# Pooled attention and a SiLU layer on one core: the first denominators two steps later, h sums in halves, another block order at the end, the last product by token halves

## The chip, the cores and the metric

The kernel runs on one core of one Trainium2 chip. The metric is the device time of one execution in microseconds (us). Three executions of the kernel before took 281.76, 282.05 and 282.42 us; the median is 282.05. TensorE is called PE, VectorE DVE, ScalarE ACT, GpSimd POOL and SyncE SP, as in the profile; PEld is PE's loading of weights.

## The reference

Eight batches with eight heads of 576 positions of 64 features. Keys and values are averaged over groups of 8 positions (72 pooled positions), then softmax attention, then a two-layer network on the 4608 rows of 512 features:

```
k_p, v_p = mean of k, v over groups of 8 positions
attn     = softmax(q @ k_p^T / sqrt(64));   x = (attn @ v_p) as [4608, 512]
h        = x @ w_in                         # [4608, 2048]
out      = (h * sigmoid(h)) @ w_out         # [4608, 512], float32
```

## The kernel before, in words

**Tiles.** The 4608 rows are nine token tiles of 512 (t = 0 to 8). While the network works on tile t, the attention of batch a = t + 1 is computed beside it, for tiles up to 6 (a < B = 8). Tiles 7 and 8 have no attention beside them; they are called bare.

**Seven products.** From tile 1 on, both layers use the seven-product form of the 2 x 2 block product (Winograd's form of Strassen). The first layer has four units a, b, c, d, each of seven products numbered 1 to 7; "a5" in the order strings is product 5 of unit a (L575 `unit_product`). The second layer has products P1 to P7 with eight blocks of depth (kt), written as "P5 Q5": P5 is kt 0 to 3, Q5 is kt 4 to 7 (L588 `out_product`). For each kt there are two matmuls of 128x256, one for each token half c of a 256-token block. One such kt, like one output half of a unit product, is a *step*.

**Accumulators.** Each of the second layer's products adds into one of three PSUM banks: o_psA (products 1, 2), o_psE (5, 3), o_psB (6, 7, 4). Between them stand operations of other engines (L601 `behind`): after product 1, DVE copies o_psA into o_psB (L605); after product 5, ACT copies o_psE into an SBUF tile p (L608); after product 6, DVE writes o_psE = o_psB + p (L610). Results go to SBUF in L632 `second`: L635 (product 2), L637 (product 3), L641 (product 7) and L646 (product 4). L482 `store` issues the output DMAs, most of them from SP's queue.

**Banks.** PSUM has eight banks in two rotating pools: "mm" with 3, "at" with 5 (L89). o_psA, o_psB and o_psE and the units' u_psB take from "mm"; u_psA, u_psE and everything of the attention take from "at".

**Sums of h.** The activated first layer lies in h_T. The seven-product form needs four sums of blocks of it, h_sum 0 to 3, made by DVE in `hidden_sum` (L532, instructions at L537). Product 5 reads sum 0, product 6 sum 1, product 7 sum 2, product 3 sum 3. Sum 1 needs sum 0, and sum 3 needs sum 1. Sum 0 needs, for its second half (kt 4 to 7), the activation of product d4, the last of the first layer.

**The order of the work.** All engines run their instructions in the program's order. The order of PE's products is a string (FOUR, BARE, THREE at L768 to L779). The rest are *fillers*, given with a step number: `spread` (L396) issues a filler with number s after the matmuls of step s, before those of step s + 1. In tile 1 (order THREE) most numbers are 2 higher. In tiles 2 to 6, steps 54 to 61 are product 1, 62 and 63 d4, 64 to 71 product 2, 72 to 79 product 5, 80 to 87 product 6, 88 to 95 product 7. In the bare tiles product 1 is 52 to 59, d3 and d4 60 to 63, P2 64 to 67, product 5 68 to 75, product 6 76 to 83, Q2 84 to 87, product 7 from 88.

**Attention in three visits.** For each third of the positions (a *visit*), `scores` (L322) makes 16 matmuls (L330) and four exponentials on ACT (L338, tile es), `denominators` (L342) four matmuls of ones with es (L348), then on ACT ln (L357) and exp(-ln) (L358), and `numerators` (L361) matmuls (L374) and products on DVE (L383) that give xT of the next tile. Ahead of the first scores of a tile, ACT loads another function table (L390), and at the tile's end it loads the other back (L393). Scores of the three visits are at steps 63, 75, 94 and denominators at 75, 87, 103 (L882); numerators of the first visit, and in tiles 2 to 6 those of the third visit of the batch before, at 87.

**The end.** In tile 8 product 7 is added and stored (L641), then product 3 (L637), then product 4 is copied by DVE (L646) and stored by two DMAs, one for each 128 tokens, one from SP's and one from ACT's queue. All stores of tile 8 are single DMAs, since its rows are contiguous.

Of the kernel before, what the change touches and what calls it, by code (L numbers as in the profile page):

```python
# [27 lines left out]
FP32 = mybir.dt.float32  # L28
# [8 lines left out]
def kernel(  # L37
# [11 lines left out]
    B, H, S, D = q.shape  # L49
# [5 lines left out]
    KF = d_model // 128  # L55
    KG = d_ff // 128
    NTT = 512
    NT = NTOK // NTT
    HS = S // 2

    KQ, NQ, CQ = KG // 2, NTT // 2, d_model // 2
# [29 lines left out]
    def ps_tile(shape, dtype, tag, name):  # L91
        return psum.tile(shape, dtype, tag=tag, bufs=banks[tag], name=name)
# [303 lines left out]
    def spread(fillers, n):  # L396
        todo = sorted(fillers, key=lambda f: f[0])
        for i in range(n):
            yield i
            while todo and todo[0][0] <= i:  # L400
                todo.pop(0)[1]()
        for f in todo:
            f[1]()
# [146 lines left out]
    def left(n, kt, c):  # L550
        cs = slice(128 * c, 128 * (c + 1))
        if n in S_OF:
            return h_sum[S_OF[n]][:, kt, cs]
        return h_block(*A_OF[n], kt, kt + 1)[:, 0, cs]
# [4 lines left out]
    def f32_tile(tag, bufs):  # L559
        return mid.tile([128, 2, 256], FP32, tag=tag, bufs=bufs, name=tag)  # L560

    def tile_products(t, order, fillers, last=False):
        order = order.split()
        step = spread(fillers, sum(KF if it[0] == "g" else 4 if it[0] in "PQ" else 2 for it in order))
        add = ALU.add
        tt, vcopy, acopy = nc.vector.tensor_tensor, nc.vector.tensor_copy, nc.scalar.copy
        ps, f32 = {}, {}

        def bank(y, b):
            tag = "mm" if y == "o" or b == "B" else "at"  # L570
            ps[y, b] = ps_tile([128, 2, 256], FP32, tag, f"{'o' if y == 'o' else 'u'}_ps{b}")

        BANK = {1: "A", 2: "A", 5: "E", 3: "E", 6: "B", 7: "B", 4: "B"}

        def unit_product(y, n):  # L575
            if n in (1, 5):
                bank(y, BANK[n])
            w, x = unit_weights(y, n), unit_x(t, n)
            for u in range(2):
                next(step)  # L580
                for kk in range(2):
                    nc.tensor.matmul(  # L582
                        ps[y, BANK[n]][:, u, :], lhsT=w[:, kk, 128 * u : 128 * (u + 1)],
                        rhs=x[:, kk, :], start=n in (1, 5) and u == 0 and kk == 0,
                        stop=kk == 1, skip_group_check=True,
                    )

        def out_product(n, k0, k1):  # L588
            if n in (1, 5) and k0 == 0:
                bank("o", BANK[n])  # L590
            w = right(n)
            for kt in range(k0, k1):
                next(step)
                for c in range(2):
                    nc.tensor.matmul(  # L595
                        ps["o", BANK[n]][:, c, :], lhsT=left(n, kt, c), rhs=w[:, kt, :],
                        start=n in (1, 5) and kt == 0 and c == 0,
                        stop=kt == KQ - 1, skip_group_check=True,
                    )

        def behind(y, n):  # L601

            if n == 1:
                bank(y, "B")
                vcopy(out=ps[y, "B"], in_=ps[y, "A"])  # L605
            elif n == 5:
                f32[y] = f32_tile("p5", 3)
                acopy(f32[y], ps[y, "E"])  # L608
            elif n == 6:
                tt(out=ps[y, "E"], in0=ps[y, "B"], in1=f32[y], op=add)  # L610

        def hidden(y, i, j, src):
            g = UNITS[y][i]
            nc.scalar.activation(  # L614
                h_T[:, g : g + 2, j * NQ : (j + 1) * NQ], src, func=AF.Silu
            )

        def unit(y, n):
            unit_product(y, n)
            behind(y, n)  # L620
            if n == 2:
                hidden(y, 0, 0, ps[y, "A"])
            elif n == 3:
                hidden(y, 1, 0, ps[y, "E"])
            elif n == 7:
                c22 = f32_tile("c22", 2)
                tt(out=c22, in0=ps[y, "B"], in1=f32[y], op=add)  # L627
                f32[y, 2] = c22
            elif n == 4:
                hidden(y, 0, 1, ps[y, "B"])  # L630

        def second(n):  # L632
            behind("o", n)
            if n == 2:
                vcopy(out=o_sb[0][:, :, LO], in_=ps["o", "A"])  # L635
            elif n == 3:
                vcopy(out=o_sb[0][:, :, HI], in_=ps["o", "E"])  # L637
                for c in range(2):
                    store(t, c, FULL)
            elif n == 7:  # L640
                tt(out=o_sb[1][:, :, HI], in0=ps["o", "B"], in1=f32["o"], op=add)  # L641
                if last:
                    for c in range(2):
                        store(t, 2 + c, HI)
            elif n == 4:
                (vcopy if last else acopy)(o_sb[1][:, :, LO], ps["o", "B"])  # L646
                for c in range(2):
                    if last:
                        store(t, 2 + c, LO, (both[c],))
                    else:  # L650
                        store(t, 2 + c, FULL)

        for it in order:
            if it[0] == "g":
                plain(t, step, int(it[1:]), 0, NTT)
            elif it[0] in "PQ":
                h = it[0] == "Q"
                out_product(int(it[1]), 4 * h, 4 * h + 4)
                if h:
                    second(int(it[1]))  # L660
            else:
                y = "abcd".index(it[0])
                if it[1] == "s":
                    hidden(y, 1, 1, f32.pop((y, 2)))
                else:
                    unit(y, int(it[1]))
        for _ in step:
            pass
# [95 lines left out]
    def load_half_2(name, half):  # L764
# [6 lines left out]
        " cs d3 c4 " + HEAD  # L771
    )
    BARE = FOUR[: FOUR.index("d3")] + (
        "c4 P1 ds Q1 d3 d4 P2 P5 Q5 P6 Q6 Q2 P7 Q7 P3 Q3 P4 Q4"
    )
    THREE = (
        "g0 g1 g2 g3 b1 b5 c1 c5 b6 b2 c6 c2 b7 b3 c7 c3 bs d1 d5 b4 cs c4 d6 d2 P1 d7 d3 Q1"
# [4 lines left out]
    for t in range(NT):  # L782
        a = t + 1
# [40 lines left out]
            continue  # L824

        order = ORDER.get(t, FOUR if a < B else BARE)
        o = 2 if t == 1 else 0
        f = []

# [3 lines left out]
        def late(s, fn, *args, **kw):  # L833
            at(s + o, fn, *args, **kw)
# [6 lines left out]
        else:  # L841
            late(43, hidden_sum, 2, 0, 4)
            late(53, hidden_sum, 2, 4, 8)
        late(64, hidden_sum, 0, 0, 4)
        late(65, hidden_sum, 0, 4, 8)
        late(66, hidden_sum, 1, 0, 8)
        late(88 if t == 1 else 76, hidden_sum, 3, 0, 8)
        if t == 1:
            for i in range(PW):
# [1 line left out]
        if a < B:  # L851
            if t == 1:
                for j in range(2):
                    at(14, slot_sums, "k", j, halves=True)
                    at(30, select_k, 2, j)
                    at(31, copy_k, 2, j)
                    late(66, slot_sums, "v", j, halves=True)
                for fn in (select_v, copy_v):
                    for j in range(2):
                        late(82, fn, 2, j, *(("at",) if fn is select_v else ()))  # L860
                at(15, load_one, 3, "k")
                at(15, load_q, 3)
                at(16, load_rest, 3, "k")
                late(64, load_one, 3, "v")
                late(66, load_rest, 3, "v")
            else:
                at(0, behind_x_sums)
                at(0, pool_k, a)
                if a + 1 < B:
                    at(0, load_one, a + 1, "k")  # L870
                at(1, pool_v, a)
                if a + 1 < B:
                    at(1, load_one, a + 1, "v")
                    at(2, load_q, a + 1)
                    at(3, load_rest, a + 1, "k")
                    at(4, load_rest, a + 1, "v")
                at(34, k_transpose, a)
            q_at = (24, 25, 26, 60) if t == 1 else (22, 32, 47, 67)
            for n in range(4):
                at(q_at[n], q_transpose, a, n % 2, n // 2)  # L880
            late(63, attn_tables)
            for n, (sc, den) in enumerate(zip((63, 75, 94), (75, 87, 103))):  # L882
                late(den, denominators, a, visits[n])
                late(sc, scores, a, visits[n])
            nu_at = (87, 103, 106)
            for n, sg in enumerate(visits):
                if n < 2 or t >= B - 2:
                    late(nu_at[n], numerators, a, sg)
                if n == 0 and 1 < t < B - 1:
                    late(nu_at[n], numerators, a - 1, visits[2])  # L890
# [33 lines left out]
```

## Time and profile before

| stage (us from the span's start) | length, us | PE busy | DVE busy | ACT busy |
|---|---|---|---|---|
| tile 2, 82.12 to 110.98 | 28.86 | 28.80 | 21.68 | 22.25 |
| tile 3, 110.98 to 139.84 | 28.86 | 28.80 | 21.75 | 22.26 |
| tile 4, 139.84 to 168.71 | 28.87 | 28.82 | 22.41 | 22.25 |
| tile 5, 168.71 to 197.51 | 28.80 | 28.75 | 21.70 | 22.26 |
| tile 6, 197.51 to 226.87 | 29.36 | 29.30 | 22.54 | 22.25 |
| tile 7, 226.87 to 251.65 | 24.78 | 24.78 | 17.76 | 13.06 |
| tile 8, 251.65 to 276.45 | 24.80 | 24.79 | 16.29 | 13.06 |
| end, 276.45 to 280.60 | 4.15 | 0.00 | 0.69 | 0.00 |

The profiled execution took 282.42 us; its span, from first to last instruction, is 280.60, with 1.82 around it. The clock granted to PE is full (1.00) in all these stages. Matmuls overlap, so a row of the timeline that gives "1.91 us x16" is a product whose successor starts 1.75 us after it. The timeline gives start, duration, engine, line, operation, and in brackets how long the engine had been idle before it and what ended that.

### The profile page before, as it was taken

What the parts mean: (1) busy time and instruction counts of PE and PEld (TensorE: products, weight loads), DVE (VectorE), ACT (ScalarE), POOL (GpSimd) and SP (SyncE); (2) the same over time, 40 slices, a digit from 0 to 9 for tenths busy, and PEclk for the clock granted to TensorE, in tenths of its full rate; (3) what the DMA queues carried; (4) which work ended last, traced back from release to release, by engine and by line L of the source; (5) the groups of instructions that cost most, each with busy time, mean ns of one, the idle gap of its engine ahead of it and who ended that gap; (6) DMA issues with size and microseconds to landing.
All of it is one profiled execution on the core that took longest, in us unless ns stands there. A gap on an engine that the chain in (4) does not pass through costs nothing.

```text
span 280.6 us, 7263 instructions
## 1 busy us (share of the span) xinstructions
PE 272.3 (97%) x2952; PEld 211.8 (75%) x2959; DVE 209.3 (75%) x377; ACT 190.5 (68%) x375; POOL 97.4 (35%) x102
## 2 busy tenths in 40 slices
PE   8889999999999999999999999999999999999994
PEld 4348544488788878887888778877887788888883
DVE  4787777887897867876787687777787687766762
ACT  1677766568669785978498858885798578319700
POOL 8565116342138510962087229850900000000000
PEclk9999999999999999999999999999999999999999
DMA  7999999896646896569546966998410032004004
GB/s 212 274 250 239 207 309 183 244 194 112 137 66 145 220 166 114 134 164 167 93 109 180 171 93 162 182 106 128 121 31 0 4 90 62 2 25 124 5 2 150
DMA packets 31473, 37.72 MB, mean 134 GB/s; under 512 B 10352, under 2 KB 22384, under 8 KB 31440
## 3 DMA queue, kind: packets, MB, share of 16 engines
q0 software_dynamic: 23792, 26.64, 52.0%
q1 hardware_dynamic: 7216, 9.97, 12.9%
q10 hardware_dynamic: 432, 0.66, 0.6%
q8 instruction: 23, 0.38, 0.6%
q14 instruction: 10, 0.08, 0.1%
HBM read 36.70 MB, written 9.44 MB: 164 GB/s over the span
## 4 chain that ended last, share of the span: by engine, by line
PE 82%; ACT 8%; DVE 3%; DMA 3%; issue 1%; POOL 1%; DVEq 0%; POOLq 0%
PE o_psB L595 16%; PE u_psB L582 15%; PE u_psA L582 10%; PE u_psE L582 10%; PE o_psE L595 8%; PE hp_ps L474 6%; PE o_psA L595 6%; ACT es L338 3%; PE o_ps L509 3%; DMA raw<-in_v_dram 3%; ACT L390 3%; PE sc_ps L330 3%; PE nu_ps L374 3%; PE den_ps L348 2%; ACT h_T L614 1%
## 5 line engine op out<-in xcount | busy, mean ns | idle before, releaser
L595 PEld LDWEIGHTS <-h_sum 128*128 128x128 bf16 x512 | 48.4, 98 | 8.9 <-issue 1.5
L582 PEld LDWEIGHTS <-w_sum 128*128 128x128 bf16 x496 | 48.2, 98 | 5.8
L338 ACT ACTIVATE es<-sc_ps 72x384 bf16<-72x384 f32 (+1 forms) x100 | 39.1, 470 | 12.9 <-PE sc_ps L330 12.8
L595 PEld LDWEIGHTS <-h_T 128*128 128x128 bf16 x384 | 36.5, 98 | 6.4 <-issue 1.4
L582 PEld LDWEIGHTS <-w_in_sb 128*128 128x128 bf16 x372 | 36.3, 98 | 4.5
L582 PE MATMUL u_psA<-xT,w_in_sb 128*128 128x256 bf16 x248 | 37.4, 273 | 0.0
L582 PE MATMUL u_psB<-x_sum,w_sum 128*128 128x256 bf16 x248 | 36.7, 272 | 0.0
L595 PE MATMUL o_psB<-w_sum,h_sum 128*128 128x256 bf16 x256 | 31.8, 273 | 0.3 <-DVE o_psE L610 0.3
L595 PE MATMUL o_psA<-w_out_sb,h_T 128*128 128x256 bf16 x256 | 31.0, 272 | 0.0
L605 DVE COPY u_psB<-u_psA 128x512 f32<-128x512 f32 x31 | 21.4, 698 | 10.4 <-PE u_psA L582 10.3
L610 DVE TENSOR_TENSOR u_psE<-u_psB,p 128x512 f32<-128x512 f32 x31 | 21.0, 694 | 9.8 <-ACT p L608 7.8
L614 ACT ACTIVATE h_T<-u_psE 128x512 bf16<-128x512 f32 x31 | 18.5, 598 | 11.2 <-PE u_psE L582 10.9
L383 DVE TENSOR_TENSOR xT<-nu_ps,rec 128x384 bf16<-128x384 f32 (+1 forms) x50 | 23.8, 533 | 0.2
L183 POOL TENSOR_TENSOR raw<-raw 72x1024 f32<-72x1024 f32 x10 | 23.6, 2361 | 0.0
L627 DVE TENSOR_TENSOR c<-u_psB,p 128x512 f32<-128x512 f32 x31 | 21.1, 682 | 3.1 <-PE u_psB L582 2.3
L614 ACT ACTIVATE h_T<-u_psB 128x512 bf16<-128x512 f32 x31 | 18.6, 600 | 4.4 <-PE u_psB L582 4.4
L537 DVE TENSOR_TENSOR h_sum<-h_T 128x1024 bf16<-128x1024 bf16 (+1 forms) x31 | 21.1, 699 | 0.4 <-ACT h_T L614 0.4
L357 ACT ACTIVATE lnd<-den_ps 128x384 f32<-128x384 f32 (+1 forms) x23 | 11.2, 485 | 14.4 <-PE den_ps L348 14.4
L614 ACT ACTIVATE h_T<-c 128x512 bf16<-128x512 f32 x31 | 19.8, 637 | 0.0
L614 ACT ACTIVATE h_T<-u_psA 128x512 bf16<-128x512 f32 x31 | 18.8, 608 | 1.2 <-PE u_psA L582 1.0
L537 DVE TENSOR_TENSOR h_sum<-h_T,h_sum 128x2048 bf16<-128x2048 bf16 x16 | 19.4, 1216 | 0.1
L474 PE MATMUL hp_ps<-xT,w_in_sb 128*128 128x288 bf16 (+2 forms) x122 | 18.8, 303 | 0.2
(83 smaller groups left out, 467.1 us busy)
## 6 DMA issues: line engine op xcount, KB each, us to landing
out_dram<-o_sb SPq DMA_DIRECT2D x128, 64.0 KB, 1.7
raw<-in_k_dram POOLq DMA_DIRECT2D x10, 576.0 KB, 8.4
raw<-in_v_dram POOLq DMA_DIRECT2D x10, 576.0 KB, 7.8
q_bf<-in_q_dram POOLq DMA_DIRECT2D x6, 576.0 KB, 9.1
w_in_sb<-in_moe_w_in_dram POOLq DMA_DIRECT2D x8, 256.0 KB, 8.6
w_out_sb<-in_moe_w_out_dram POOLq DMA_DIRECT2D x4, 512.0 KB, 13.4
raw<-in_v_dram POOLq DMA_DIRECT2D x2, 768.0 KB, 11.6
raw<-in_k_dram POOLq DMA_DIRECT2D x1, 768.0 KB, 10.0
```

The lines of the kernel that those rows point to most:

```text
L183: nc.gpsimd.tensor_add(out=raw[:, :, : 2 * D], in0=raw[:, :, : 2 * D], in1=raw[:, :, 2 * D :])
L338: nc.scalar.activation(es[:, s, :], sc[s], func=AF.Exp, scale=score_scale)
L357: nc.scalar.activation(lnd, den_ps[:, :w], func=AF.Ln)
L383: nc.vector.tensor_mul(out=xT[:, 2 * g0 + c : 2 * (g0 + ng - 1) + c + 1 : 2, cols], in0=nu[c][:, :w].rearrange("r (g n) -> r g n", g=ng), ...
L474: nc.tensor.matmul(hp_ps[:, r0:r1], lhsT=w_in_sb[:, kk, g * 128 : (g + 1) * 128], rhs=xT[:, kk, x0 : x0 + r1 - r0], start=(kk == 0), stop= ...
L537: nc.vector.tensor_tensor(out=h_sum[n][:, k0:k1, :], in0=get(a), in1=get(b), op=op)
L582: nc.tensor.matmul(ps[y, BANK[n]][:, u, :], lhsT=w[:, kk, 128 * u : 128 * (u + 1)], rhs=x[:, kk, :], start=n in (1, 5) and u == 0 and kk == 0,
L595: nc.tensor.matmul(ps["o", BANK[n]][:, c, :], lhsT=left(n, kt, c), rhs=w[:, kt, :], start=n in (1, 5) and kt == 0 and c == 0, stop=kt == K ...
L605: vcopy(out=ps[y, "B"], in_=ps[y, "A"])
L610: tt(out=ps[y, "E"], in0=ps[y, "B"], in1=f32[y], op=add)
L614: nc.scalar.activation(h_T[:, g : g + 2, j * NQ : (j + 1) * NQ], src, func=AF.Silu)
L627: tt(out=c22, in0=ps[y, "B"], in1=f32[y], op=add)
```

## The change

It has five parts. The denominators of the first visit and the scores of the second go from step 75 to 77. Sum 1 of h is made in two halves; in tiles 2 to 7 its first half goes ahead of the second half of sum 0, and in the bare tiles first halves are issued at earlier steps. In the bare tiles P2, product 5, product 6, Q2 become: one step of product 5, three of product 2, the rest of product 5, product 6, the rest of product 2 (in tile 8 two and two steps), and o_psE takes a bank from "at". In tile 8, o_psB is replaced by two banks from "at", one for each token half, and the operations on it are made by halves. The last product is computed for one token half, which ACT copies and whose store goes out from ACT's queue, and then for the other, with DVE and SP's queue.

```diff
+    def steps(it):
+        if it[0] == "o":
+            k0, k1 = it[3:].split("-")
+            return int(k1) - int(k0)
+        return KF if it[0] == "g" else 4 if it[0] in "PQRS" else 2
...
+        bare = t + 1 >= B
         def bank(y, b):
-            tag = "mm" if y == "o" or b == "B" else "at"
+            tag = "mm" if (y == "o" and not (bare and b == "E")) or b == "B" else "at"
...
+        def o_bank(n, c):
+            b = BANK[n]
+            return ps["o", f"B{c}" if last and b == "B" else b][:, c, :]
+
+        def out_product(n, k0, k1, cs=(0, 1)):
...
+                if len(cs) == 2 or kt % 2 == 0:
+                    next(step)
+                for c in cs:
                     nc.tensor.matmul(
+                        o_bank(n, c), lhsT=left(n, kt, c), rhs=w[:, kt, :],
...
         def second(n):
-            behind("o", n)
-            if n == 2:
+            if not last or n in (2, 3, 5):
+                behind("o", n)
+            if n == 1 and last:
+                for c in range(2):
+                    ps["o", f"B{c}"] = ps_tile([128, 2, 256], FP32, "at", "o_psB")
+                    vcopy(out=o_bank(6, c), in_=ps["o", "A"][:, c])
+            elif n == 2:
...
+            elif n == 6 and last:
+                for c in range(2):
+                    tt(out=ps["o", "E"][:, c], in0=o_bank(6, c), in1=f32["o"][:, c], op=add)
             elif n == 7:
-                tt(out=o_sb[1][:, :, HI], in0=ps["o", "B"], in1=f32["o"], op=add)
                 if last:
                     for c in range(2):
+                        tt(
+                            out=o_sb[1][:, c, HI], in0=o_bank(7, c), in1=f32["o"][:, c],
+                            op=add,
+                        )
                         store(t, 2 + c, HI)
+                else:
+                    tt(out=o_sb[1][:, :, HI], in0=ps["o", "B"], in1=f32["o"], op=add)
...
+            elif it[0] == "o":
+                n, (k0, k1) = int(it[1]), map(int, it[3:].split("-"))
+                out_product(n, k0, k1)
+                if k1 == KQ:
+                    second(n)
+            elif it[0] in "RS":
+                c = "RS".index(it[0])
+                out_product(int(it[1]), 0, KQ, (c,))
+                (vcopy if c else acopy)(o_sb[1][:, c, LO], o_bank(4, c))
+                store(t, 2 + c, LO, (both[1 - c],))
...
     BARE = FOUR[: FOUR.index("d3")] + (
-        "c4 P1 ds Q1 d3 d4 P2 P5 Q5 P6 Q6 Q2 P7 Q7 P3 Q3 P4 Q4"
+        "c4 P1 ds Q1 d3 d4 o5:0-1 o2:0-3 o5:1-8 P6 Q6 o2:3-8 P7 Q7 P3 Q3 P4 Q4"
     )
...
         order = ORDER.get(t, FOUR if a < B else BARE)
+        if t == NT - 1:
+            order = order.replace("P4 Q4", "R4 S4").replace("o5:0-1 o2:0-3 o5:1-8", "o5:0-2 o2:0-2 o5:2-8").replace("o2:3", "o2:2")
...
-        late(64, hidden_sum, 0, 0, 4)
+        late(64 if a < B else 57, hidden_sum, 0, 0, 4)
+        late(66 if t in (1, NT - 1) else 64 if a < B else 62, hidden_sum, 1, 0, 4)
         late(65, hidden_sum, 0, 4, 8)
-        late(66, hidden_sum, 1, 0, 8)
+        late(66, hidden_sum, 1, 4, 8)
...
-            for n, (sc, den) in enumerate(zip((63, 75, 94), (75, 87, 103))):
+            for n, (sc, den) in enumerate(zip((63, 77, 94), (77, 87, 103))):
```

## The prediction

> **What bounds the kernel now.** I read the page's shares first, then the chain of waits in order of time, then the timeline around every place where the chain leaves TensorE (PE), and last the stage table and the DMA shares at the end.
>
> ```profile
> PE 272.3 (97%) x2952; PEld 211.8 (75%) x2959; DVE 209.3 (75%) x377; ACT 190.5 (68%) x375; POOL 97.4 (35%) x102
> PE 82%; ACT 8%; DVE 3%; DMA 3%; issue 1%; POOL 1%; DVEq 0%; POOLq 0%
> ```
>
> PE is the bound. So only PE's holes count, and what follows PE's last matmul. The chain shows an undisturbed product of 16 matmuls as 1.75 us, or 0.109 us a matmul, 0.22 a step (two matmuls). What a product takes beyond that is a hole. From the timeline of tile 6:
>
> ```profile
> 212.26 1.28 ACT L390 ACT_TABLE_LOAD   x1
> 213.56 1.62 ACT L338 ACTIVATE es<-sc_ps 72x384 bf16<-72x384 f32 x4
> ...
> 214.75 0.81 PE L348 MATMUL den_ps<-es,ones 72*32 72x384 bf16 x4
> ...
> 215.48 0.54 PE L330 MATMUL sc_ps<-qT,kz 32*72 32x192 bf16 x16
> 215.59 0.49 ACT L357 ACTIVATE lnd<-den_ps 128x384 f32<-128x384 f32 x1 [0.41 <-PE den_ps L348]
> ...
> 216.55 1.60 ACT L338 ACTIVATE es<-sc_ps 72x384 bf16<-72x384 f32 x4
> ...
> 218.03 0.59 ACT L608 COPY p<-o_psE 128x512 f32<-128x512 f32 x1
> 218.68 0.10 PEld L348 LDWEIGHTS <-ones 72*32 72x32 bf16 x4 [0.21 <-issue]
> 218.68 0.35 PE L348 MATMUL den_ps<-es,ones 72*32 72x384 bf16 x4
> ...
> 218.86 0.70 DVE L610 TENSOR_TENSOR o_psE<-o_psB,p 128x512 f32<-128x512 f32 x1 [2.46 <-PE o_psB L595]
> ```
>
> See two things. The first visit's four denominator matmuls take 0.81 us, the second's 0.35: the fourth must wait for the last exponential (213.56 + 1.62 = 215.18). The hole is 0.46 us, and the first denominators show 0.81 in each of tiles 1 to 6. Second, ACT runs almost without a break from the table load to the copy p, which stands behind the second visit's exponentials; L610 needs p and, in a bare tile too, frees o_psB for product 7.
>
> The bare tiles 7 and 8 have two holes each, between d4 and product 2 and before product 7 (tile 7):
>
> ```profile
> 240.10 0.70 DVE L605 COPY o_psB<-o_psA 128x512 f32<-128x512 f32 x1 [0.70 <-PE o_psA L595]
> ...
> 240.85 1.03 PE L595 MATMUL o_psA<-w_out_sb,h_T 128*128 128x256 bf16 x8
> ...
> 241.59 0.69 DVE L537 TENSOR_TENSOR h_sum<-h_T 128x1024 bf16<-128x1024 bf16 x1 [0.20 <-ACT h_T L614]
> ```
>
> Product 2 writes o_psA, which L605 reads until 240.80. d4's matmuls start at 240.27, so product 2 could have started at 240.27 + 4 x 0.109 = 240.71: hole 0.14. In the same way product 7 starts at 246.25, 0.14 late, since L610 ends at 245.50 + 0.70 = 246.20.
>
> **Part 1, denominators and second scores two steps later (tiles 1 to 6).** The filler moves past two steps, 4 x 0.109 = 0.44 us of PE work. Denominators start at 214.75 + 0.44 = 215.19, as the last exponential ends, and finish where they did, 215.55. The scores start at 215.48 as before, so ACT's whole chain (ln, reciprocal, second exponentials, p) keeps its clock times, while PE is 0.44 ahead. No DMA moves with it, and no other allocation from the five-bank pool is passed, so the bank rotation stays.
>
> What is late next: p still ends at 218.03 + 0.59 = 218.62. L610 was set by PE (218.86); PE now offers product 6 at 218.42, but p holds L610 to 218.65, and it ends at 219.35. Product 7, which started at 219.62 behind the numerators with L610 just done (219.56), would want 219.18 and gets 219.40. Queued behind it on PE is everything up to the tile's end, so the tile keeps 0.22, less than half the hole. Tiles 2 to 5 show the same numbers (tile 5: p ends 189.81, L610 starts 190.05, slack 0.24): **5 x 0.21 = 1.05**. After that PE leads again (third exponentials: ACT idle 1.61 for PE), so nothing gives it back. Tile 1 differs: no extra numerators follow, p ends at 74.10, L610 starts at 74.69 and would be PE-led at 74.25: **0.44**. Bounds: 0.14 to 0.44 a tile.
>
> **Part 2, h sums in halves.** Sum 1 of 1.22 us becomes two of 0.68 (the 128x1024 row): 0.14 more on DVE a tile. Cover in tiles 2 to 6: DVE idles 2.46 before L610. Sum 0's second half ends one half-sum later, at 213.17 + 0.68 = 213.85; product 5's fifth step now wants it at 214.66. Cost 0; without the cover 6 x 0.14 = 0.84. A rule against this is in the Trainium skill, "VectorE: DVE Perf Modes", section on the TRN2 errata: a fixed cost falls on each instruction, so tile to 512 elements or more. By it alone all the halves would be loss, some 0.15 us each (an estimate from its 150 cycles at 0.96 GHz); the rows agree on the size, yet place it in DVE's idle time.
>
> **Part 3, block order of tiles 7 and 8.** Product 5's first step(s) now cover L605, and five or six steps of product 2 (1.09, 1.31 us) cover L610: both 0.14 holes close. But product 5's fifth step comes earlier. It reads sum 0's second half, ready at 241.59 + 0.69 = 242.28 because it waits for d4's activation on ACT, and no edit moves that. In tile 7 seven steps precede it: 240.71 + 14 x 0.109 = 242.24; the weight load (0.10) starts after the sum, so the matmul gets 242.42. From there 4 + 8 + 5 steps of 0.218 bring product 7 to 246.13, against 246.25: gain 0.12. In tile 8 (d4 at 265.06) only six precede it: wanted at 265.06 + 16 x 0.109 = 266.80, the sum is ready at 266.38 + 0.69 = 267.07, matmul at 267.21; 4 + 8 + 6 steps give 271.14 against 271.04: loss 0.10. Together **0.02**; bounds -0.3 to +0.56. o_psE's new bank was last used by unit b or c, finished long before. Half copies and half adds at 0.42 (row 128x256, 0.424) fit under those steps.
>
> **Part 4, the end.**
>
> ```profile
> 276.48 0.69 DVE L646 COPY o_sb<-o_psB 128x512 f32<-128x512 f32 x1 [1.05 <-PE o_psB L595]
> 277.20 0.37 ACTq L486 DMA_DIRECT2D out_dram<-o_sb  x1
> ```
>
> The first token half now ends eight matmuls (0.87) earlier and ACT copies it (72x256 row: 0.37), issue near 276.0; the second is a DVE copy of 0.42, issue at 276.93 instead of 277.20. But the DMA shares say the engines are full with two 256 KB stores from 276.29 to 277.67, then with the last two (128 KB each) from 278.06 to 278.83. Busy 1.38 + 0.77 = 2.15; packed without the hole they end at 276.29 + 2.15 = 278.44: **gain 0.39**. Bounds: 0.27 (only the copy is shorter) to 0.65 (the last store unhindered: 277.20 to first packet 278.06 is 0.86, so 277.79 + 0.385). The 1.77 from last packet to the end of the span stays. "DMA: Bandwidth & Descriptors", section "Issuing engines are not separate DMA queues", says that queues share the 16 engines and a second one saves only issue time; by that alone the gain would be near 0 for the queue and 0.27 for the copy. What I count is the earlier start.
>
> **Sum.** 1.05 + 0.44 + 0.02 + 0.39 = 1.90 us. The profiled execution took 282.42 (span 280.60 and 1.82 around it): 280.52. It is the highest of the three runs; from their median 282.05 I get **280.15**. The unit costs hold alike for both.
>
> **Rivals.**
> (a) Product 7 is not held by p, for instance because ACT's chain also moves up: all six tiles keep 0.44, 2.64 + 0.02 + 0.39 = 3.05, so 279.0. Against it: p's place behind the exponentials, whose start is bound by the table load. 14%.
> (b) Little is left: if denominators end about 0.2 later than computed (PE's change of shape costs 0.21 of weight-load idle there), p and L610 follow and tiles 2 to 6 keep 0; tile 1 still gives 0.44, and if the end gains nothing for want of DMA, 0.46 in all: 281.6. 16%.
> (c) Slower: the 0.46 is not the wait for the exponentials but stays with the denominators wherever they are. They then end 0.44 later, p ends at 219.06, L610 at 219.79, product 7 starts at 219.84 against 219.62: five tiles lose 0.22, tile 1 nothing; 1.10 less 0.41 from parts 3 and 4 is 0.69 lost: 282.74. It decides once the denominators end over 0.41 late. Against it: the second visit's 0.35. 6%.
> The forecast itself has 64%, its own range 279.6 to 281.0.
>
> **How the numbers follow.** The range reaches from (a) to short of (b): 279.0 to 281.5. About 0.2% (0.56 us) is what a measurement of this kernel can tell from no change: faster 0.64 + 0.14 = 0.78, same 0.16, slower 0.06.
>
> **What would show it.** Right: first denominators at 0.35 in six tiles; ln at the same distance from the table load; a wait of product 7 on L610 of about 0.2 in tiles 2 to 6; tiles 2 to 6 shorter by 0.2; product 5 waiting for h_sum in tiles 7 (0.2) and 8 (0.4); no hole between the last DMA bursts. Wrong: tiles shorter by 0.44 with no wait before product 7, or denominators still at 0.8.

## The result and the profile after

The changed kernel takes 280.10 us (median of four runs, 279.64 to 280.23) beside 281.94 for the kernel before in the same measurement: ratio 0.9929, 95% interval 0.9911 to 0.9947. The prediction from the median was 280.15. The profiled execution took 280.23 us; its span is 278.45 us (280.65 before; the pages round these to 278.4 and 280.6).

Where the 2.2 us of the two spans came from, by the first matmul of each tile in the timelines (tile 8 up to the end of its last matmul). The table ahead of the prediction cuts where the last matmul of the tile before ends, 0.16 us after the first matmul of the next has started, so tile 8 has 24.80 there.

| stage | before, us | after, us | gain | predicted |
|---|---|---|---|---|
| start and tile 0 (tile 1 begins at 55.58, 55.29) | 55.58 | 55.29 | 0.29 | not part of the change |
| tile 1 | 26.38 | 25.94 | 0.44 | 0.44 |
| tiles 2 to 6 | 144.74 | 143.88 | 0.86 | 1.05 |
| tile 7 | 24.79 | 24.59 | 0.20 | 0.12 |
| tile 8 | 24.95 | 24.98 | -0.03 | -0.10 |
| end | 4.21 | 3.77 | 0.44 | 0.39 |

The change's own stages give 1.91 us. The 0.29 at the start is scatter: in the profiles of the twelve kernels of this study, which all share the program up to there, tile 1 begins between 54.78 and 55.59, 0.8 us apart. The later stages repeat within some 0.05.

The page after, shares of the engines and of the chain:

```profile
PE 270.7 (97%) x2952; PEld 212.4 (76%) x2959; DVE 209.6 (75%) x388; ACT 190.6 (68%) x376; POOL 97.3 (35%) x102
PE 87%; ACT 6%; DVE 4%; issue 1%; DVEq 0%
```

PE has the same matmuls and stays the bound. Tile 6 in the timeline after (L608 is the old L595, L618 the old L605, L621 the old L608, L623 the old L610, L627 the old L614):

```profile
212.13 1.62 ACT L338 ACTIVATE es<-sc_ps 72x384 bf16<-72x384 f32 x4
...
213.75 0.37 PE L348 MATMUL den_ps<-es,ones 72*32 72x384 bf16 x4
214.05 0.54 PE L330 MATMUL sc_ps<-qT,kz 32*72 32x192 bf16 x16
214.23 0.49 ACT L357 ACTIVATE lnd<-den_ps 128x384 f32<-128x384 f32 x1 [0.48 <-PE den_ps L348]
...
216.66 0.59 ACT L621 COPY p<-o_psE 128x512 f32<-128x512 f32 x1
216.81 0.35 PE L348 MATMUL den_ps<-es,ones 72*32 72x384 bf16 x4
216.98 0.83 PE L374 MATMUL nu_ps<-es,vp 72*32 72x192 bf16 x32
217.28 0.70 DVE L623 TENSOR_TENSOR o_psE<-o_psB,p 128x512 f32<-128x512 f32 x1 [2.24 <-PE den_ps L348]
...
218.04 1.69 PE L608 MATMUL o_psB<-w_sum,h_sum 128*128 128x256 bf16 x14 [0.22 <-DVE o_psE L623]
```

The denominators take 0.37 for 0.81: that hole is gone. A new one stands before product 7: it starts 218.04 - 216.98 = 1.06 after the numerators, where it was 219.62 - 218.85 = 0.77 before. That is 0.29 us of waiting (the row's 0.22 counts only the time that PE stands idle). What L623 waits for is named by the list of waits (who waited for whom: us in total, times, longest), first before, then after:

```profile
DVE o_psE L610 <- PE o_psB L595: 14.3, 8, 2.5
...
PE o_psB L595 <- DVE o_psE L610: 0.3, 1, 0.3
```

```profile
DVE o_psE L623 <- ACT p L621: 9.3, 5, 2.2
...
PE o_psB L608 <- DVE o_psE L623: 1.4, 6, 0.3
```

Before, it was product 6 in all eight tiles, and PE waited for L610 once, in tile 1. After, it is p in tiles 1 to 5. In tile 6 the row names the second denominators; p ends at 216.66 + 0.59 = 217.25, 0.03 before L623, and is the other thing that came last.

Tile 7 after, then tile 8:

```profile
238.44 0.70 DVE L618 COPY o_psB<-o_psA 128x512 f32<-128x512 f32 x1
...
239.11 0.38 PE L608 MATMUL o_psE<-w_sum,h_sum 128*128 128x256 bf16 x2
...
239.33 0.82 PE L608 MATMUL o_psA<-w_out_sb,h_T 128*128 128x256 bf16 x6
...
239.99 0.69 DVE L537 TENSOR_TENSOR h_sum<-h_T 128x1024 bf16<-128x1024 bf16 x1 [0.26 <-ACT h_T L627]
...
240.74 2.52 PEld L608 LDWEIGHTS <-h_sum 128*128 128x128 bf16 x24 [0.22 <-DVE h_sum L537]
```

```profile
264.58 0.60 PE L608 MATMUL o_psE<-w_sum,h_sum 128*128 128x256 bf16 x4
264.58 0.69 DVE L537 TENSOR_TENSOR h_sum<-h_T 128x1024 bf16<-128x1024 bf16 x1 [0.79 <-ACT h_T L627]
...
265.33 2.52 PEld L608 LDWEIGHTS <-h_sum 128*128 128x128 bf16 x24 [0.43 <-DVE h_sum L537]
265.33 1.05 PE L608 MATMUL o_psE<-w_sum,h_sum 128*128 128x256 bf16 x8 [0.16 <-DVE h_sum L537]
```

Product 5 starts right behind d4 (239.11), so L618 is covered. Its fifth step waits for the second half of sum 0, which waits for ACT, in both tiles. In tile 8 it was due at 264.58 + 4 x 0.109 = 265.02 and runs at 265.33.

The end after:

```profile
273.84 0.37 ACT L687 COPY o_sb<-o_psB 128x256 f32<-128x256 f32 x1 [6.78 <-PE o_psB L608]
274.24 0.35 ACTq L486 DMA_DIRECT2D out_dram<-o_sb  x1
274.71 0.42 DVE L687 COPY o_sb<-o_psB 128x256 f32<-128x256 f32 x1 [1.05 <-PE o_psB L608]
```

The last copy is 0.42 for 0.69, the first half's store goes out at 274.24, before the last matmul ends (274.68). By their shares the DMA engines are busy without a hole from 274.54 to 276.71: in steps of 0.2 us the share is 0.29 from 274.4, then 0.90 to 1.10, and 0.53 from 276.6.

### The profile page after: what moved, and what is told of

It is laid out like the page before. It is cut to its first block, busy times and chain, and to the rows that moved or that the text cites. A ratio compares the mean times of both kernels' runs of the same rounds, so it can differ in the third digit from the quotient of the medians.

```text
span 278.4 us, 7274 instructions
## 1 busy us (share of the span) xinstructions
PE 270.7 (97%) x2952; PEld 212.4 (76%) x2959; DVE 209.6 (75%) x388; ACT 190.6 (68%) x376; POOL 97.3 (35%) x102
## 4 chain that ended last, share of the span: by engine, by line
PE 87%; ACT 6%; DVE 4%; issue 1%; DVEq 0%
PE u_psB L589 14%; PE o_psB L608 13%; PE o_psA L608 10%; PE u_psA L589 10%; PE u_psE L589 10%; PE o_psE L608 9%; PE hp_ps L474 6%; PE o_ps L509 3%; PE sc_ps L330 3%; ACT es L338 3%; PE warm_ps L708 2%; PE den_ps L348 2%; DVE o_psE L623 2%; PE nu_ps L374 1%; DVE xT L383 1%; ACT rec L358 1%
## 5 line engine op out<-in xcount | busy, mean ns | idle before, releaser
L608 PEld LDWEIGHTS <-h_sum 128*128 128x128 bf16 x512 | 48.7, 98 | 10.1 <-issue 2.2
L608 PEld LDWEIGHTS <-h_T 128*128 128x128 bf16 x384 | 36.5, 98 | 6.1 <-issue 1.1
L608 PE MATMUL o_psB<-w_sum,h_sum 128*128 128x256 bf16 x256 | 31.8, 273 | 1.4 <-DVE o_psE L623 1.4
L608 PE MATMUL o_psA<-w_out_sb,h_T 128*128 128x256 bf16 x256 | 31.0, 272 | 0.0
L618 DVE COPY u_psB<-u_psA 128x512 f32<-128x512 f32 x31 | 21.4, 697 | 10.5 <-PE u_psA L589 10.3
L623 DVE TENSOR_TENSOR u_psE<-u_psB,p 128x512 f32<-128x512 f32 x31 | 20.9, 693 | 9.7 <-ACT p L621 8.6
L627 ACT ACTIVATE h_T<-u_psE 128x512 bf16<-128x512 f32 x31 | 18.5, 597 | 11.2 <-PE u_psE L589 11.0
L627 ACT ACTIVATE h_T<-u_psB 128x512 bf16<-128x512 f32 x31 | 18.6, 600 | 4.4 <-PE u_psB L589 4.4
L537 DVE TENSOR_TENSOR h_sum<-h_T,h_sum 128x1024 bf16<-128x1024 bf16 (+1 forms) x24 | 20.4, 858 | 0.1
L627 ACT ACTIVATE h_T<-c 128x512 bf16<-128x512 f32 x31 | 19.7, 637 | 0.0
L627 ACT ACTIVATE h_T<-u_psA 128x512 bf16<-128x512 f32 x31 | 18.8, 607 | 1.2 <-PE u_psA L589 1.0
```

What stands on the lines that cost most here:

```text
L537: nc.vector.tensor_tensor(out=h_sum[n][:, k0:k1, :], in0=get(a), in1=get(b), op=op)
L608: nc.tensor.matmul(o_bank(n, c), lhsT=left(n, kt, c), rhs=w[:, kt, :], start=n in (1, 5) and kt == 0 and c == 0, stop=kt == KQ - 1, skip_g ...
L627: nc.scalar.activation(h_T[:, g : g + 2, j * NQ : (j + 1) * NQ], src, func=AF.Silu)
```

## The experiments

The theory and its rivals stand with each run. All ratios are to the kernel before, measured beside it. The lengths of tiles and ends come from the profiles, one execution for each kernel.

**1. The move of the denominators alone.**

```diff
-            for n, (sc, den) in enumerate(zip((63, 75, 94), (75, 87, 103))):
+            for n, (sc, den) in enumerate(zip((63, 77, 94), (77, 87, 103))):
```

> The kernel before with one line changed: first denominators and second scores at step 77, nothing else. Theory (PE gets 0.44 us ahead in each of tiles 1 to 6, and in tiles 2 to 6 the copy p on ACT holds L610 and so product 7 for 0.2 of it): 0.44 + 5 x 0.17 = 1.3 us faster, ratio 0.9954; product 7 shows a wait of 0.2 on L610. Rival (the denominators' hole is not the wait for the exponentials): their row stays at 0.8 us and the time does not fall. Rival (the gain of the whole change comes from the other parts): under 0.5 us faster.

Measured: 280.64 us beside 281.97, 1.33 faster, ratio 0.9949 (0.9935 to 0.9963). Tiles 2 to 6 are 28.70, 28.69, 28.70, 28.64, 29.20 long, 0.16 or 0.17 less than before, tiles 7 and 8 as before; tile 1 is 25.94 for 26.38; together 1.26. The list of waits has product 7 on L610 six times, 1.4 us in all, as in the whole change. One line gives about 1.3 of the 1.84.

**2. Halves and the bare tiles alone.** Besides these lines it has o_psE's bank from "at" in the bare tiles and, in tile 8, two steps of product 5 and two of product 2 at the place of one and three.

```diff
-        "c4 P1 ds Q1 d3 d4 P2 P5 Q5 P6 Q6 Q2 P7 Q7 P3 Q3 P4 Q4"
+        "c4 P1 ds Q1 d3 d4 o5:0-1 o2:0-3 o5:1-8 P6 Q6 o2:3-8 P7 Q7 P3 Q3 P4 Q4"
...
-        late(64, hidden_sum, 0, 0, 4)
+        late(64 if a < B else 57, hidden_sum, 0, 0, 4)
+        late(66 if t in (1, NT - 1) else 64 if a < B else 62, hidden_sum, 1, 0, 4)
         late(65, hidden_sum, 0, 4, 8)
-        late(66, hidden_sum, 1, 0, 8)
+        late(66, hidden_sum, 1, 4, 8)
```

> The whole change without the move to step 77 and with the old end (product 4 in one piece, o_psB whole): h sums in halves, and the new block order and o_psE bank in tiles 7 and 8. Theory: tiles 1 to 6 as before; tile 7 0.18 us shorter, tile 8 as long as before, because the two holes of 0.14 close and product 5 waits for the second half of sum 0 (0.2 in tile 7, 0.4 in tile 8): 0.2 us faster, ratio 0.9993. Rival (both holes of both tiles close and nothing takes their place): 0.56 us faster, ratio 0.998.

Measured: ratio 0.9993 (0.9985 to 1.0001), too small a difference for the device time. The stages are sharper: tile 7 is 24.60 for 24.79, tile 8 24.97 for 24.95. The rival's 0.56 is out.

**3. The end alone.** Besides these lines it has the new order of the last product, the two banks for o_psB in tile 8 and the operations on it by halves.

```diff
+                out_product(int(it[1]), 0, KQ, (c,))
+                (vcopy if c else acopy)(o_sb[1][:, c, LO], o_bank(4, c))
+                store(t, 2 + c, LO, (both[1 - c],))
```

> The kernel before with the new end alone: in tile 8 o_psB in two banks with operations by halves, and the last product by token halves, each stored as it is ready. Theory: tiles 1 to 8 as before, and from the last matmul to the end of the span 3.7 us for 4.15: 0.4 us faster, ratio 0.9985. Rival (only the shorter last copy counts): 0.27 us. Rival (the last stores are hidden behind the two 256 KB stores): 0.

Measured: ratio 0.9991 (0.9979 to 1.0002); its interval alone decides nothing. From the last matmul to the end of the span it is 3.78 us for 4.21, a gain of 0.43 and more than the 0.27 of the first rival. Tile 8 is 25.00 for 24.95.

**4. The copy p taken off ACT.** Added to the whole change; it runs only in tiles 2 to 6.

```diff
-                acopy(f32[y], ps[y, "E"])
+                (vcopy if y == "o" and 1 < t < B - 1 else acopy)(f32[y], ps[y, "E"])
```

> The whole change, and in tiles 2 to 6 the copy p of product 5 (L621) by DVE instead of ACT. Theory (p's place behind the second exponentials on ACT is what holds product 7): L623 starts when product 6 is done, product 7 waits no more, each of five tiles gains a further 0.2 us: 1.1 us faster than the whole change, some 279.0 us, ratio to before 0.990. Rival (something else holds product 7, such as the numerators or DVE): no gain, or some 0.1 a tile lost to DVE's 0.69 us copy, ratio 0.993 to 0.995.

Measured: 278.41 us, ratio 0.9873 (0.9857 to 0.9889), below the whole change's interval. Its tile 3:

```profile
128.52 0.69 DVE L621 COPY p<-o_psE 128x512 f32<-128x512 f32 x1
128.53 1.60 ACT L338 ACTIVATE es<-sc_ps 72x384 bf16<-72x384 f32 x4
130.16 0.35 PE L348 MATMUL den_ps<-es,ones 72*32 72x384 bf16 x4
130.27 0.70 DVE L623 TENSOR_TENSOR o_psE<-o_psB,p 128x512 f32<-128x512 f32 x1 [1.05 <-PE o_psB L608]
130.33 0.83 PE L374 MATMUL nu_ps<-es,vp 72*32 72x192 bf16 x32
...
131.10 1.70 PE L608 MATMUL o_psB<-w_sum,h_sum 128*128 128x256 bf16 x14
```

DVE's copy stands beside the exponentials, L623 is released by product 6, and product 7 starts 131.10 - 130.33 = 0.77 after the numerators: the wait is gone. Each of the five tiles is 0.27 or 0.28 shorter than in the whole change (28.37, 28.42, 28.43, 28.36, 28.92), 1.38 in all. So p's place on ACT was the holder, and what it held is 0.28 a tile, not the 0.2 expected.

**5. d4 ahead of d3 in the bare tiles.** Added to the whole change.

```diff
-        "c4 P1 ds Q1 d3 d4 o5:0-1 o2:0-3 o5:1-8 P6 Q6 o2:3-8 P7 Q7 P3 Q3 P4 Q4"
+        "c4 P1 ds Q1 d4 d3 o5:0-1 o2:0-3 o5:1-8 P6 Q6 o2:3-8 P7 Q7 P3 Q3 P4 Q4"
```

> The whole change, and in tiles 7 and 8 product d4 ahead of d3. Theory (what product 5's fifth step waits for is d4's activation, by way of the second half of sum 0): that half comes 0.4 us earlier, the waits of 0.2 in tile 7 and 0.4 in tile 8 go, the two tiles together are 0.5 to 0.6 us shorter, some 279.5 us. Rival (the wait is for DVE, busy with sum 1 and the half copies): no gain, or the wait moves to another product.

Measured: 279.93 us, ratio 0.9926 (0.9913 to 0.9940); the device time can't tell it apart from the whole change's 280.10. Tile 8:

```profile
264.11 0.69 DVE L537 TENSOR_TENSOR h_sum<-h_T 128x1024 bf16<-128x1024 bf16 x1 [0.30 <-ACT h_T L627]
...
264.59 1.47 PE L608 MATMUL o_psE<-w_sum,h_sum 128*128 128x256 bf16 x12
```

Twelve matmuls of product 5 run without a break. Tile 7 is 24.48 for 24.59, tile 8 24.65 for 24.98: 0.44 together, so the waits were 0.11 and 0.33. The mechanism holds, the expected 0.5 to 0.6 was too much.

**6. Tile 7's order in tile 8 too.**

```diff
-            order = order.replace("P4 Q4", "R4 S4").replace("o5:0-1 o2:0-3 o5:1-8", "o5:0-2 o2:0-2 o5:2-8").replace("o2:3", "o2:2")
+            order = order.replace("P4 Q4", "R4 S4")
```

> The whole change with tile 7's order (one step of product 5, three of product 2) in tile 8 as well. Theory: product 5's fifth step comes one step later, so it waits 0.2 us less, and five steps of product 2 still cover the half adds: tile 8 is 0.2 us shorter than in the whole change, 24.6 for 24.8. Rival (the half copies and half adds need the two and six steps): tile 8 as long or longer.

Measured (one execution): tile 8 is 24.76 for 24.98, 0.22 shorter. One step more ahead of product 5's fifth is worth its 0.22, and five steps still cover the half adds.

**7. Without the two large stores of tile 8.** The first 256 rows of the tile are not written.

```diff
-                for c in range(2):
+                for c in range(2 if not last else 0):
                     store(t, c, FULL)
```

> The whole change without the two 256 KB stores of tile 8 (its first 256 rows are not written). Theory (the DMA engines are full from these stores to the last one, and that sets the end): the end from the last matmul falls from 3.7 to 3.4 us. Rival (the last copy, the issue and a fixed delay set the end): it stays at 3.7.

Measured (one execution): the end is 3.11 us beside 3.77, less than either expected. DMA shares (the column before the last; the last is GB/s):

```profile
276.00:276.20 0.20, 0.00 (x0) 0.00 (x0) 0.00 (x0) 0.00 (x0) 0.00 (x0) 1.00 0.81 287
276.20:276.40 0.20, 0.00 (x0) 0.00 (x0) 0.00 (x0) 0.00 (x0) 0.00 (x0) 1.00 0.95 323
276.40:276.60 0.20, 0.00 (x0) 0.00 (x0) 0.00 (x0) 0.00 (x0) 0.00 (x0) 1.00 0.16 46
```

By the shares the last store is done at 276.43, 0.28 earlier than in the whole change (the last matmuls of the two end within 0.01 of each other): that is the expected part. The rest lies behind it. In the traces' records of single packets the last one ends at 276.53, at 276.80 in the whole change and at 278.93 before; to the end of the span that leaves 1.27, 1.65 and 1.72 us, and 1.64 to 1.75 in the other nine profiles. So the end also gains some 0.4 us behind the last packet. What makes that difference was not tried.

**8. Both last stores on SP's queue.**

```diff
-                store(t, 2 + c, LO, (both[1 - c],))
+                store(t, 2 + c, LO, (both[0],))
```

> The whole change with both last stores on SP's queue. Theory (the queues share full DMA engines, so only the order of the bytes changes): the end from the last matmul stays at 3.7 us within 0.1. Rival (the second queue is what gives the gain): 4.0.

Measured (one execution): the end is 3.77 us, as in the whole change. The second queue gives nothing here; the engines are full either way, from 274.11 to 276.29.

**9. Halves of sum 1 alone, tiles 1 to 6.**

```diff
+        if a < B:
+            late(66 if t == 1 else 64, hidden_sum, 1, 0, 4)
         late(65, hidden_sum, 0, 4, 8)
-        late(66, hidden_sum, 1, 0, 8)
+        late(66, hidden_sum, 1, 4 if a < B else 0, 8)
```

> The kernel before with sum 1 of h in halves in tiles 1 to 6 alone, its first half ahead of sum 0's second half in tiles 2 to 6. Theory (0.06 to 0.14 us more on DVE a tile lies in DVE's 2.4 us of idle time before L610): no difference, ratio 1.000. Rival (it delays what PE waits for): 0.1 a tile, 0.6 us slower.

Measured: ratio 1.0002 (0.9992 to 1.0013), and the tiles are 28.80, 28.85, 28.86, 28.80, 29.35 against 28.86, 28.86, 28.86, 28.80, 29.35. The halves cost nothing. Tile 2 is even 0.06 shorter, as in run 2 (28.80): a hole in the first layer's products, 10.7 us into the tile, is gone. Why is not shown.

**10. p on DVE and d4 first together** (the edits of runs 4 and 5).

> The whole change with p made by DVE in tiles 2 to 6 and d4 ahead of d3 in tiles 7 and 8. If both theories hold, the two gains add, since they lie in different tiles: 1.4 us in tiles 2 to 6 (0.28 a tile in the run with p on DVE) and 0.5 in tiles 7 and 8, some 278.1 us, ratio to before 0.986. Rival (one takes from the other, by DVE's work or by the banks): under 1.5 us in all against the whole change.

Measured: 278.21 us, ratio 0.9865 (0.9847 to 0.9883), against the changed kernel's 0.9911 to 0.9947. In the stages both gains are there in full (28.36 to 28.91 in tiles 2 to 6 as in run 4, 24.48 and 24.65 in tiles 7 and 8 as in run 5), 1.82 in all. By device time the gain on the whole change is 1.89, where run 4 alone gave 1.69. The two profiled executions, 278.44 and 278.46, hardly differ, since tile 1 begins at 55.34 here and at 54.90 in run 4, which hides the 0.44. This version has the lowest median here; its interval overlaps that of run 4.

## Why the prediction was right

- **Part 1, the stall and its removal: shown.** The row went from 0.81 to 0.37, and run 1 got 1.33 us from that line alone.
- **Part 1, what is late next: shown.** "p holds L610" was the step that set the size. Run 4 took p away from ACT, changed nothing else, and the wait went. Without this step the forecast would have been rival (a), 279.0.
- **Part 1, the size: 0.21 a tile was 0.16** (run 1). The mis-sized term is p's time: the prediction said that ACT's chain "keeps its clock times". By the records the denominators do end where they did, 0.37 us after the last exponential (ends of matmuls are modelled), but ln begins 0.48 after it (213.75 to 214.23), for 0.41 before (215.18 to 215.59). p follows by 0.06, so product 7 waits 0.29, not 0.22. Before, the row began 0.43 ahead of the last exponential's end; now it begins with it, so all four matmuls lie behind. That this makes the 0.07 is inferred from the rows and was not tried alone.
- **Part 1, tile 1: 0.44, as computed.** There L623 starts at 73.96, 0.12 after product 6's last matmul (72.59 + 1.25 = 73.84), as L610 did before (74.69 after 73.32 + 1.26 = 74.58); p ends just ahead, at 73.87. Product 7's wait of 0.25 on it was there before as well and moved along.
- **Part 2: no cost, as predicted**, by run 9. Two halves also take less than the counted 2 x 0.68: back to back they take 1.28 us (69.42 in the timeline after) for 1.22 in one piece. The 0.06 in tile 2 was not foreseen.
- **Part 3, mechanism right, size too small: 0.02 was 0.17.** Both holes closed and product 5 waits for sum 0, as computed. The mis-sized term is the 0.14 from the end of the sum to the matmul, with a weight load of 0.10 in it. In tile 8 load and matmul start together at 265.33, 0.06 after the sum ends (264.58 + 0.69 = 265.27); in tile 7 the load starts at 240.74, again 0.06 after (239.99 + 0.69 = 240.68). The prediction had 0.18 and 0.41 for the waits; run 5 shows 0.11 and 0.33.
- **Part 4: 0.39 was 0.44.** The packing of the last transfers is what the shares show, 2.17 us of unbroken work for the computed 2.15. By the packets' records the last one ends 2.12 us after the last matmul (276.80 - 274.68) for 2.49 (278.93 - 276.44): 0.37 of the 0.39. The other 0.07 lies behind the last packet, where 1.65 us pass for 1.72. The prediction read that stretch as 1.77 from the shares and let it stay; this is its mis-sized term. Run 8 shows that the second queue has no part in the gain.

The close total owes something to luck: part 1 was 0.23 too high (1.26 in run 1 for 1.49), parts 3 and 4 were 0.20 too low, and the rest is tile 2's 0.05 or 0.06 that no part foresaw.

## What to carry to other kernels

When a stall is taken out, follow the engine that caused it to its next delivery: here ACT's chain kept its times to 0.06 us, and a plain copy further down its queue took back nearly two thirds of the gain in five tiles (0.28 of 0.44 us). An engine with idle time just there (DVE) was the place for that copy, and moving it was worth 1.38 us beside the 1.91 of the whole change. Gains of 0.2 us in a run of 280 are settled by stage lengths from the profile, not by the device time, whose scatter sat in the start.

## What was not expected of the hardware

- The time from the last packet to the end of the span is not a constant: it was 1.27 us in run 7 (one execution), where two large stores less were ahead of it and the DMA engines had paused, and 1.64 to 1.75 in the eleven other profiles. Which of the two matters is not shown.
- Halving costs less on DVE than a second row of that size suggests: two copies of 128x256 back to back take 0.77 us (tile 8, L651 in the timeline after), one of 128x512 0.70; the separate row of 0.42 would have made it 0.84.
- A weight load that was held up by its operand does not add its 0.10 to the matmul behind it in the record: in tile 8 both start 0.06 us after the operand is ready, while undisturbed the load leads its matmul by 0.11 (264.47 and 264.58).
